# Four batches of sketch attention and routed expert attention: from stages with gaps to one written list for three engines

## The chip, the cores and the metric

The kernel runs on one core of one Trainium2 chip. The metric is the device time of one execution in microseconds (us). Engines are named as in the profile: PE is TensorE's matmuls and PEld its weight loads, DVE is VectorE, ACT is ScalarE, POOL is GpSimd and SP is SyncE, which here only issues DMAs.

## The reference

Inputs are q, k, v of (4 batches, 4 heads, 1088 rows, 32), two 8 x 32 sketch matrices S1 and S2 in 64-bit floats, and the weights of a routed attention layer with four experts of width 64. In outline:

```
a, b  = S1 x, S2 x                        # for every row x of q and of k
phi   = outer(a, b)                       # 64 features for one head
kv, z = sum_s phi(k) v, sum_s phi(k)
x     = phi(q) kv / (phi(q) z + 1e-6)     # heads side by side: 128 columns
logits = x @ w_gate;  the top 2 of 4 experts, softmax over the two
for each expert e:
    scores = x wq[e] (x wk[e])^T / 8, causal;  a = softmax(scores)
    ye = a (x wv[e]) wo[e]
    out += weight of e in this row * ye
```

## The kernel before

Rows are cut into nine tiles of 128 (tiles 0 to 7) and 64 (tile 8). One batch goes through these pieces, each a function of the kernel:

- `begin_k`, `begin_q`: DVE transposes of the loaded k and q. `sketch`: PE multiplies 64-row halves with the sketch weights `SKW`, which are split into a high and a low 32-bit part (NS is 2); the two parts accumulate in PSUM over two matmuls of 32 columns. ACT copies out, and one product makes the 64 features (`kp`, `qp`): on DVE in batch 0, on POOL afterwards.
- `kvs` sums phi(k) v over the rows. `turn_features` transposes the features of q on PE. `numer` multiplies and DVE divides, which gives `xs`; `turn_x` transposes it to `xT`. `spread_x` copies `xs` by 16 DMAs into `xrep`, the left operand of `values`.
- `gate`: one matmul of 4 columns for each tile, with the 128 columns of `xT` as the weights; then DVE finds the chosen two experts (`sel`), and `weights()` makes their shares (`gw`) with steps on DVE, POOL and ACT.
- `chosen`: x times all four expert matrices wq wk^T (512 columns), from which ACT copies two blocks and DVE overwrites parts by predicate, so that `u` holds for each row the vectors of its two chosen experts. `turn_chosen` transposes `u` to `uT`.
- `step` (and `last_step` for tile 8): the scores of both chosen experts, 128 i + 128 columns for tile i; DVE takes them out of PSUM with the mask and the minimum (`take`), ACT makes the exponentials and their sums (`soften`), and DVE transposes the weights block by block into `aT` (`turns`).
- `values`: for each block of 32 keys, four matmuls of 32 rows (one for each quarter of a block, each into its own PSUM bank) of `xrep` with `aT`. `keep` copies the sums to `yT` by one ACT instruction.
- `Out.heads`, `Out.turn`, `Out.put`: the value projections of the chosen experts, scaled on DVE (`hb`) and added on POOL; a PE transpose; the output projection, an ACT copy and the output DMAs.

Order. PE, DVE and ACT run each its instructions in the order in which the Python code emits them. For each batch the loop goes over six score steps, (4,2), (5,1), (3), (6,0), (7), (8). After each step's matmuls, takes and exponentials come the transposes of the step before, and then a list of other work for that gap (`gaps_of`): the output of the batch before, the sketches and features of the next. `values` of the groups B (tiles 4, 5) and C (tiles 1, 2, 3) stand in one gap, those of group A (0, 6, 7, 8) in the first gap of the next batch. The eight PSUM banks are divided: banks 0 to 3 belong to the scores alone, and `bank()` goes round banks 4 to 7 for all else; `values` takes all four of these.

Of the kernel before, what the change touches and what calls it, by code (L numbers as in the profile page):

```python
# [15 lines left out]
AX = mybir.AxisListType  # L16


@with_exitstack
def kernel(  # L20
# [15 lines left out]
    nc = tc.nc  # L36
# [145 lines left out]
    ident = const("ident", [128, 128])  # L184
    make_identity(nc, ident)
# [16 lines left out]
    GROUPS = {"B": (4, 5), "C": (1, 2, 3), "A": (0, 6, 7, 8)}  # L202
    COL = {"B": 0, "C": 128, "A": 0}
    KEPT = {"B": 0, "C": 4, "A": 10}
# [70 lines left out]
    def sketch(b, nm, j0, j1, eng):  # L275
# [5 lines left out]
        k0 = bank(2)  # L281
        for j in range(j0, j1):
            for m in range(2):
                for half in (0, 64):
                    rows, x = slice(64 * m, 64 * m + 64), 128 * j + half
                    for s in range(NS):
                        nc.tensor.matmul(P[half : half + 64, k0 + m, 32 * (j - j0) : 32 * (j - j0) + 32],  # L287
                                         xT_[rows, x : x + 64],
                                         SKW[rows].rearrange("p s x h r -> p (s x h r)")[:, 32 * s : 32 * s + 32],
                                         start=(s == 0), stop=(s == NS - 1))  # L290
        for m in range(2):
            t = P[:, k0 + m, 0 : 32 * (j1 - j0)].rearrange("p (j x d) -> p x j d", j=j1 - j0, x=2)
            nc.scalar.copy(ab[:, :, j0:j1, 2 * m : 2 * m + 2].rearrange("p x j h r -> p x j (h r)"), t)  # L293
# [62 lines left out]
    def gate(b, j0, j1):  # L356
        m_, k0 = batch(b), bank()
        for j in range(j0, j1):
            nc.tensor.matmul(P[:, k0, E * j : E * j + E], m_.xT[:, 128 * j : 128 * j + 128], wg, start=True, stop=True)
# [20 lines left out]

        def weights():
            V.reduce_max(top.rearrange("p j o -> p (j o)"), lg, axis=AX.X)
            G.tensor_tensor(out=w, in0=lg, in1=tops, op=ALU.subtract)
            nc.scalar.activation(out=w, in_=w, func=ACTF.Exp)
            G.tensor_tensor(out=w, in0=w, in1=ch, op=ALU.mult)
# [3 lines left out]
            G.tensor_tensor(out=w, in0=w, in1=tops, op=ALU.mult)  # L389
# [3 lines left out]
        return weights  # L393

    def chosen(b, i):
# [29 lines left out]
    def step(b, tiles):  # L425
# [8 lines left out]
        for s in range(2):  # L434
            for i in tiles:
                c, end = at[i], at[i] + 128 * i + 128
                while c < end:
                    n = min(end, c // 512 * 512 + 512) - c
                    nc.tensor.matmul(flat[:, 1024 * s + c : 1024 * s + c + n], m_.uT[:, i, s],  # L439
                                     m_.xT[:, c - at[i] : c - at[i] + n], start=True, stop=True)  # L440
                    c += n
        for s in range(2):
            for x, i in enumerate(tiles):
# [3 lines left out]
                take(a[:, s, cols], flat[:, 1024 * s + at[i] : 1024 * s + at[i] + n], mask[:, 1024 - n :], m)  # L447
                soften(a[:, s, cols], m, m_.z[:, i, s : s + 1])

        def turns():  # L450
            for i in tiles:
                n, u0 = blocks(i), unit(i)
                nc.vector.transpose(aT[GRP[i]][:, 0:n, u0 : u0 + 2].rearrange("p c s k -> p s c k"),  # L453
                                    a[:, :, at[i] : at[i] + 32 * n].rearrange("p s (c k) -> p s c k", k=32))

        return turns

    def last_step(b):

        m_, k0, i = batch(b), bank(), NJ - 1  # L460
# [237 lines left out]
```

## Time and profile before

| | us |
|---|---|
| three timed runs | 474.12, 480.95, 484.09 (median 480.95) |
| the profiled execution, its own time | 478.73 |
| its span, first to last instruction | 476.8 |
| PE, DVE, ACT, POOL busy | 381.3, 196.1, 136.7, 62.7 |

The profiled execution lies 2.2 us below the median, and 1.9 us of its time lie around its span. Busy is the time in which an engine's records run; a busy PE is not PE at its peak, since the granted clock has two levels (1.2 and 2.4 GHz) and was 0.846 of the upper one on average.

### The profile page before, as it was taken

To read this page: it belongs to the slowest core of one execution; us is meant where nothing else is said; L and a number is where in the kernel's file an instruction comes from. 1 tells how busy PE (TensorE), PEld (TensorE's weight loads), DVE (VectorE), ACT (ScalarE), POOL (GpSimd) and SP (SyncE) were. 2 spreads that over 40 slices of the span, in tenths; PEclk is the share of its full clock that TensorE was granted. 3 is DMA by queue.
4 is the path that set the end of the run, shared out by engine and by line. 5 is a ranking of instruction groups with operands and counts; after the bars stand their busy time and mean duration, and the time that the engine had idled before them with its cause. 6 is when DMAs were issued, how large, how long until landed. Compare 5 with 4: busy or idle time off the path is not lost.

```text
span 476.8 us, 12480 instructions
## 1 busy us (share of the span) xinstructions
PE 381.3 (80%) x5480; PEld 280.5 (59%) x5480; DVE 196.1 (41%) x527; ACT 136.7 (29%) x352; POOL 62.7 (13%) x132
## 2 busy tenths in 40 slices
PE   5978778698876977599788786789797787788795
PEld 2963433576653945368755763568574575367584
DVE  4334454442465054531663236512455416343601
ACT  2223142232325042231333232302422413423211
POOL 2010000430101001322011001124010100000101
PEclk9555787689889898979789897859978898889899
DMA  8410431110000080300000062000000025000000
GB/s 207 126 50 1 107 83 47 49 50 3 2 1 28 6 180 21 99 3 3 3 0 29 1 138 50 21 1 4 3 2 11 18 58 132 20 3 1 5 25 21
DMA packets 30326, 19.23 MB, mean 40 GB/s; under 512 B 5184, under 2 KB 29248, under 8 KB 30272
## 3 DMA queue, kind: packets, MB, share of 16 engines
q1 hardware_dynamic: 30256, 18.43, 15.6%
q8 instruction: 43, 0.70, 0.6%
q14 instruction: 11, 0.09, 0.1%
q10 hardware_dynamic: 16, 0.00, 0.0%
HBM read 7.28 MB, written 2.23 MB: 20 GB/s over the span
## 4 chain that ended last, share of the span: by engine, by line
PE 63%; DVE 18%; ACT 8%; issue 5%; POOL 3%; DMA 2%; SPq 0%; ACTq 0%; POOLq 0%; DVEq 0%
PE P L487 18%; PE P L439 16%; PE P L398 6%; PE P L531 5%; DVE a L419 5%; DVE u L408 5%; PE P L229 4%; PE P L325 3%; PE P L309 3%; PE P L287 3%; PE P L548 3%; ACT a L423 2%; DVE aTA L453 2%; POOL kp L296 2%; PE P L466 2%
## 5 line engine op out<-in xcount | busy, mean ns | idle before, releaser
L419 DVE CUSTOM_DVE_ANT_0 a<-P,mask 128x640 f32<-128x640 f32 (+4 forms) x64 | 46.6, 756 | 116.7 <-PE P L439 116.7
L439 PE MATMUL P<-xT,uT 128*128 128x512 f32 (+3 forms) x192 | 79.3, 567 | 1.4 <-ACT uT L230 1.4
L423 ACT ACTIVATE a<-a,mx 128x512 f32<-128x512 f32 (+8 forms) x68 | 54.0, 795 | 75.3 <-DVE mx L419 75.0
L408 DVE COPY_PREDICATED u<-sel,P 128x128 f32<-128x128 int32 x144 | 31.8, 293 | 68.3 <-ACT u L404 68.3
L439 PEld LDWEIGHTS P<-xT,uT 128*128 128x128 f32 x192 | 38.4, 221 | 32.1 <-issue 26.9
L398 PE MATMUL P<-mcat,xT 128*128 128x512 f32 x72 | 46.3, 749 | 8.1 <-DVE u L408 5.1
L487 PE MATMUL P<-aTA,xrep 32*128 32x160 f32 (+3 forms) x1080 | 44.0, 318 | 8.2 <-DVE r L511 8.2
L487 PEld LDWEIGHTS P<-aTA,xrep 32*128 32x128 f32 x1080 | 43.3, 204 | 10.5 <-ACT a L423 9.9
L531 PE MATMUL P<-wvx,yT 128*128 128x192 f32 (+1 forms) x144 | 39.0, 431 | 2.2 <-ACT yT L492 1.0
L537 POOL TENSOR_TENSOR hb<-hb 128x128 f32<-128x128 f32 (+1 forms) x36 | 16.3, 454 | 150.1 <-DVE hb L535 149.8
L531 PEld LDWEIGHTS P<-wvx,yT 128*128 128x128 f32 (+1 forms) x144 | 31.4, 244 | 5.8 <-issue 3.0
L492 ACT COPY yT<-P 128x1280 f32<-128x1280 f32 (+1 forms) x8 | 8.5, 1066 | 82.2 <-PE P L487 82.2
L535 DVE TENSOR_TENSOR hb<-P,gw 128x384 f32<-128x384 f32 (+1 forms) x36 | 19.1, 549 | 28.1 <-PE P L531 27.9
L229 PE MATMUL P<-ident,u 64*128 64x64 f32 x144 | 14.6, 272 | 17.8 <-DVE u L408 16.9
L229 PEld LDWEIGHTS P<-ident,u 64*128 64x128 f32 x144 | 9.0, 145 | 32.4 <-DVE u L408 15.1
L229 PEld LDWEIGHTS P<-ident,hb 64*128 64x128 f32 x144 | 7.7, 149 | 33.8 <-POOL hb L537 19.3
L229 PE MATMUL P<-ident,hb 64*128 64x64 f32 x144 | 11.9, 257 | 17.3 <-POOL hb L537 11.4
L487 PE MATMUL P<-aTB,xrep 32*128 32x128 f32 (+1 forms) x720 | 23.4, 272 | 2.8 <-ACT qab L293 2.8
L398 PEld LDWEIGHTS P<-mcat,xT 128*128 128x128 f32 x72 | 14.5, 226 | 17.5 <-issue 9.4
L487 PEld LDWEIGHTS P<-aTB,xrep 32*128 32x128 f32 x720 | 22.8, 187 | 3.3 <-ACT qab L293 3.1
L548 PE MATMUL P<-wo,hT 128*128 128x128 f32 (+1 forms) x144 | 21.8, 293 | 3.0 <-DVE u L408 3.0
L403 ACT COPY u<-P 128x128 f32<-128x128 f32 x36 | 9.4, 262 | 51.2 <-PE P L398 51.2
(116 smaller groups left out, 470.2 us busy)
## 6 DMA issues: line engine op xcount, KB each, us to landing
xrep<-xs SPq DMA_DIRECT2D x32, 144.0 KB, 3.3
xrep<-xs SPq DMA_DIRECT2D x32, 128.0 KB, 3.2
kin<-in_k_dram SPq DMA_DIRECT2D x4, 544.0 KB, 3.8
qin<-in_q_dram SPq DMA_DIRECT2D x4, 544.0 KB, 3.9
vin<-in_v_dram SPq DMA_DIRECT2D x16, 128.0 KB, 3.9
out_dram<-ob SPq DMA_DIRECT2D x32, 64.0 KB, 1.5
vtl<-in_v_dram SPq DMA_DIRECT2D x8, 16.0 KB, 2.4
wqk<-in_moe_wq_dram SPq DMA_DIRECT2D x1, 128.0 KB
```

What stands on the lines that cost most here:

```text
L229: nc.tensor.transpose(P[:, k0 + h, 64 * x : 64 * x + 64], a[rows], ident[rows, rows])
L287: nc.tensor.matmul(P[half : half + 64, k0 + m, 32 * (j - j0) : 32 * (j - j0) + 32], xT_[rows, x : x + 64], SKW[rows].rearrange("p s x h r ...
L398: nc.tensor.matmul(P[:, k0], m_.xT[:, 128 * i : 128 * i + 128], mcat.rearrange("p e d -> p (e d)"), start=True, stop=True)
L408: V.copy_predicated(u[:, s], m_.sel[:, i, 3 * s + x : 3 * s + x + 1].bitcast(I32).to_broadcast([128, DM]), c[:, x])
L419: nc.vector.tensor_tensor_reduce(out=dst, in0=src, in1=msk, scale=-1.0, scalar=most, op0=ALU.add, op1=ALU.min, accum_out=mx)
L423: nc.scalar.activation(out=a, in_=a, func=ACTF.Exp, bias=mx, scale=-1.0, accum_out=z)
L439: nc.tensor.matmul(flat[:, 1024 * s + c : 1024 * s + c + n], m_.uT[:, i, s], m_.xT[:, c - at[i] : c - at[i] + n], start=True, stop=True)
L487: nc.tensor.matmul(P[:, 4 + r, COL[grp] + 32 * us[0] : COL[grp] + 32 * len(units)], xrep[rows, c], aT[grp][rows, c, us[0] :], start=(c == ...
L531: nc.tensor.matmul(P[0:nq, k0, 64 * X * s : 64 * X * s + 64 * X], m_.yT[:, u, quarters].rearrange("p r q -> p (r q)"), wvx[:, X * s : X * ...
L535: nc.vector.tensor_tensor(out=hb[0:nq], in0=P[0:nq, k0, 0 : 2 * X * HD].rearrange("p (x d) -> p x d", d=HD), in1=m_.gw[0:nq, i, :, None].t ...
L537: nc.gpsimd.tensor_tensor(out=hb[0:nq, 1:3], in0=hb[0:nq, 1:3], in1=hb[0:nq, 4:6], op=ALU.add)
L548: nc.tensor.matmul(P[0:nq, k0, DM * t : DM * t + DM], self.hT[:, 2 * t + g, 0:nq], wo_sb[:, g], start=(g == 0), stop=(g == NG - 1))
```

## The change

The loop over batches, steps and gaps is replaced by `ORDER`, a written list of 321 words. A word is batch, task and arguments: `1.s:4:2` is the score step of tiles 4 and 2 of batch 1. The list sets the order of PE, DVE and ACT, from the first instruction on (`manual_schedule` now covers the setup too). Tasks: bk, bq = begin_k, begin_q; ks, qs = sketch of k, q; kv = kvs; tf = turn_features; nu = numer; tx = turn_x; sp = spread_x; ld = load_next; ga = gate, ge = its exponentials, gw = the rest of its weights; c = chosen; tu = turn_chosen; s = scores; t = transposes of one tile's weights; vb, va = a quarter of `values` of a group; sh = shares; h, ht, o = heads, turn, put. The first part of the list, two later places and its end:

```
0.bk 0.ks:0:4 0.vk 0.bq1 0.ks:4:9 0.bq0 0.em 0.kv 1.ld 0.qs:4:9 0.tf:13:18 0.tf:8:13 1.bk 0.qs:0:4 0.nu:4:9
0.tf:0:8 1.bq 0.tx:4:9 0.nu:0:4 1.ks:4:9 1.ks:0:4 0.tx:0:4 0.sp 2.ld 0.ga:0:4 0.ge:0 0.c:2 0.c:3 0.c:1 1.kv
0.tu:2:3 2.bk 1.qs:4:9 0.c:0 1.qs:0:4 0.s:3 0.gw:0 2.bq 1.tf:8:13 0.tu:0:1 0.t:3 0.ga:4:9 1.tf:0:8 0.c:5 0.c:4
1.tf:13:18 2.ks:0:4 0.c:7 0.ge:4 1.nu:0:5 0.tu:4:5 0.c:6 0.c:8 0.s:5:1 0.s:4:2 1.nu:5:9 0.tu:6:7 0.tu:8 0.t:1
0.t:2 2.ks:4:9 1.tx:4:9 0.t:5 1.tx:0:4 0.s:7 0.t:4 2.kv 2.qs:4:9 2.qs:0:4 0.s:8 0.s:6:0 0.gw:4 2.tf:8:13 0.t:6
0.t:0 0.sh:0:6 3.ld 0.t:7 0.t:8 0.vb:0 2.tf:13:18 0.vb:1 0.vb:2 0.vb:3 1.ga:0:9 2.tf:0:8 0.h:4 0.va:0 1.c:3 0.va:1
...
3.sp 3.t:4 2.sh:0:6 3.t:1 3.s:7 2.h:3 3.s:8 2.h:0 2.h:4 3.s:6:0 3.vb:0 3.vb:1 3.t:6 2.ht:0 3.t:0 2.sh:6:9 3.vb:2
...
3.t:8 2.o:6 3.va:0 3.gw:0 2.o:8 3.va:1 3.sh:0:6 3.h:4 3.va:2 3.sh:6:9 3.h:3 3.va:3 3.h:2 3.ht:3 3.h:1 3.h:5 3.o:3
3.ht:1 3.h:8 3.ht:5 3.o:1 3.h:6 3.h:7 3.ht:8 3.o:5 3.h:0 3.ht:6 3.o:8 3.ht:0 3.o:6 3.o:0
```

Besides the order: `bank()` takes of all eight banks the one (or the aligned pair) that was used longest ago, except banks that a running `values` holds. Groups B and C become one group B (tiles 1 to 5), `values` runs in four parts of a group (words vb:0 to vb:3), and four copies, two on ACT and two on DVE, take its sums out. `aT` is kept in two parts for each group, so that a tile's transpose becomes up to two. `sketch` multiplies by both parts of `SKW` at once (64 columns) and DVE adds the halves. `gate` uses 32 columns of `xT` as weights in place of 128. `chosen` makes one ACT copy and two wider predicated copies. The add of `heads` and small steps of `weights` and `shares` move from POOL to DVE.

The core of the diff:

```diff
     def bank(n=1):
-        k = turn[0] % 4
-        if n == 2 and k % 2:
-            k = (k + 1) % 4
-        turn[0] = k + n
-        return 4 + k
+        k = min((k for k in range(0, 8, n) if not held & set(range(k, k + n))), key=lambda k: max(used[k : k + n]))
+        used[k : k + n] = [max(used) + 1] * n
+        return k
+    ctx.enter_context(tc.manual_schedule(
+        engines={mybir.EngineType.PE, mybir.EngineType.DVE, mybir.EngineType.Activation}))
...
-    GROUPS = {"B": (4, 5), "C": (1, 2, 3), "A": (0, 6, 7, 8)}
+    GROUPS = {"B": (1, 2, 3, 4, 5), "A": (0, 6, 7, 8)}
+    CUT = {"B": 16, "A": 4}
...
-                    for s in range(NS):
-                        nc.tensor.matmul(P[half : half + 64, k0 + m, 32 * (j - j0) : 32 * (j - j0) + 32],
-                                         xT_[rows, x : x + 64],
-                                         SKW[rows].rearrange("p s x h r -> p (s x h r)")[:, 32 * s : 32 * s + 32],
-                                         start=(s == 0), stop=(s == NS - 1))
+                    nc.tensor.matmul(P[half : half + 64, k0 + m, w * (j - j0) : w * (j - j0) + w], xT_[rows, x : x + 64],
+                                     SKW[rows].rearrange("p s x h r -> p (s x h r)"), start=True, stop=True)
...
+            nc.scalar.copy(o, t[:, 0])
+            if NS == 2:
+                nc.vector.tensor_tensor(out=o, in0=t[:, 1], in1=o, op=ALU.add)
...
-            nc.tensor.matmul(P[:, k0, E * j : E * j + E], m_.xT[:, 128 * j : 128 * j + 128], wg, start=True, stop=True)
+            for r in range(4):
+                x = 128 * j + 32 * r
+                nc.tensor.matmul(P[32 * r : 32 * r + 32, k0, E * j : E * j + E], m_.xT[:, x : x + 32], wg,
+                                 start=True, stop=True)
...
-        nc.scalar.copy(u[:, 0], c[:, 0])
-        nc.scalar.copy(u[:, 1], c[:, 3])
+        nc.scalar.copy(u, c[:, 0:4:3])
...
+            f = 512 * bank(2 if base > 512 else 1)
...
+    PARTS = {"B": (0, 4, 8, 14, 24), "A": (0, 7, 14, 21, 34)}
+    def values(b, grp, part):
+        if part == 0:
+            k0 = bank(2)
+            held.update((k0, k0 + 1))
+            k1 = bank(2)
+            held.update((k1, k1 + 1))
+            sums[grp] = k0, k0 + 1, k1, k1 + 1
...
+            for r in range(4):
+                (nc.scalar.copy, nc.vector.tensor_copy)[r % 2](
+                    batch(b).yT[:, KEPT[grp] : KEPT[grp] + n, r],
+                    P[:, sums[grp][r], 0 : 32 * n].rearrange("p (u q) -> p u q", q=32))
...
-            nc.gpsimd.tensor_tensor(out=hb[0:nq, 1:3], in0=hb[0:nq, 1:3], in1=hb[0:nq, 4:6], op=ALU.add)
+            nc.vector.tensor_tensor(out=hb[0:nq, 1:3], in0=hb[0:nq, 1:3], in1=hb[0:nq, 4:6], op=ALU.add)
...
+    for word in ORDER.split():
+        b, task = word.split(".")
+        name, *args = task.split(":")
+        TASKS[name](int(b), *map(int, args))
```

## Rows read from the trace of the kernel before

**Rows 1.** The page: busy time, share of the span and instructions of each engine.

```profile
PE 381.3 (80%) x5480; PEld 280.5 (59%) x5480; DVE 196.1 (41%) x527; ACT 136.7 (29%) x352; POOL 62.7 (13%) x132
```

**Rows 2.** Span and mean granted clock of the core.

```profile
core 0: 476.8 us, clock 0.846
```

**Rows 3.** Stages: length, busy (instructions) of PE, PEld, DVE, ACT, POOL; granted clock, DMA.

```profile
0.00:42.00 42.00, 30.98 (x493) 22.97 (x493) 17.09 (x57) 9.41 (x24) 5.80 (x25) 0.62 0.41 109
42.00:103.00 61.00, 47.10 (x562) 28.58 (x563) 28.09 (x85) 19.04 (x59) 7.74 (x14) 0.73 0.26 65
103.00:213.00 110.00, 87.01 (x1364) 65.41 (x1364) 46.92 (x123) 33.18 (x88) 17.11 (x29) 0.91 0.15 37
213.00:325.00 112.00, 92.73 (x1364) 69.64 (x1364) 46.32 (x121) 32.84 (x85) 15.42 (x26) 0.85 0.11 26
```

**Rows 4.** Waits of PE: for whom, us in total, times, longest.

```profile
PE P L229 <- DVE u L408: 16.9, 15, 2.9
PE P L229 <- POOL hb L537: 11.4, 8, 2.6
PE P L309 <- POOL kp L296: 8.8, 6, 2.7
PE P L487 <- DVE r L511: 8.2, 3, 2.7
PE P L229 <- ACT qpT L230: 7.6, 3, 2.5
```

**Rows 5.** Short stretches inside the period of batch 2, columns as in rows 3.

```profile
306.00:316.50 10.50, 8.57 (x220) 8.24 (x220) 2.29 (x2) 1.30 (x5) 4.34 (x2) 0.53 0.01 3
316.50:322.00 5.50, 5.50 (x15) 2.99 (x12) 1.31 (x4) 0.72 (x2) 0.00 (x0) 0.65 0.00 0
325.30:336.00 10.70, 10.65 (x297) 10.52 (x298) 0.00 (x0) 0.27 (x2) 4.33 (x3) 1.00 0.02 5
```

**Rows 6.** PE in order of time: start, us, line, shape, count, idle before.

```profile
203.73 0.83 PE L309 MATMUL P<-vp,kp 128*64 128x33 f32 x12
204.49 5.28 PE L439 MATMUL P<-xT,uT 128*128 128x512 f32 x12
...
218.62 4.56 PE L487 MATMUL P<-aTC,xrep 32*128 32x192 f32 x111
...
242.57 2.17 PE L359 MATMUL P<-wg,xT 128*128 128x4 f32 x18
...
259.18 3.62 PE L439 MATMUL P<-xT,uT 128*128 128x512 f32 x12
...
306.43 4.10 PE L287 MATMUL P<-SKW,kT 64*64 64x32 f32 x144
...
313.41 3.20 PE L309 MATMUL P<-vp,kp 128*64 128x33 f32 x56 [1.55 <-POOL kp L296]
...
322.03 2.36 PE L287 MATMUL P<-SKW,qT 64*64 64x32 f32 x144
```

**Rows 7.** Groups by line: count, busy us, mean ns of one, idle before.

```profile
L398 PE MATMUL P<-mcat,xT 128*128 128x512 f32 x72 | 46.3, 749 | 8.1 <-DVE u L408 5.1 <-ACT yT L492 3.0
L408 DVE COPY_PREDICATED u<-sel,P 128x128 f32<-128x128 int32 x144 | 31.8, 293 | 68.3 <-ACT u L404 68.3
L537 POOL TENSOR_TENSOR hb<-hb 128x128 f32<-128x128 f32 (+1 forms) x36 | 16.3, 454 | 150.1 <-DVE hb L535 149.8
...
L325 PE MATMUL P<-kvz,qpT 64*64 64x33 f32 x576 | 13.9, 263 | 2.3 <-ACT qpT L230 2.1
...
L332 DVE TENSOR_TENSOR xs<-P,den 128x256 f32<-128x256 f32 (+1 forms) x16 | 6.6, 453 | 0.5
...
L371 DVE TENSOR_TENSOR eq<-eq,lower 128x144 f32<-128x144 f32 (+2 forms) x5 | 1.4, 278 | 0.2
```

**Rows 8.** SP in order of time, 160 to 200 us, columns as in rows 6.

```profile
165.41 11.81 SPq L220 DMA_DIRECT2D xrep<-xs  x16
```

More of the change, by code (lines that the diff above doesn't have):

```diff
@@ L468, in last_step @@
         take(a[:, 1024:], P[:, k0, 0:64], mask_last, mx[:, 0, 0:1])
[L469 removed]
+        take(a[:, 0:1024], flat[:, 512 * k1 : 512 * k1 + 1024], mask[:, 0:1].to_broadcast([128, 1024]), mx[:, 0, 1:2],
+             mx[:, 0, 0:1])
         soften(a, mx[:, 0, 1:2], m_.z[:, i, 0:1])
[L472 to L477 removed]
+        left[b, i] = a[:, None, :]
+    PARTS = {"B": (0, 4, 8, 14, 24), "A": (0, 7, 14, 21, 34)}
+    sums = {}
+    def values(b, grp, part):
         tiles, units = GROUPS[grp], UNITS[grp]
+        if part == 0:
[4 more added lines that the diff above has]
+            sums[grp] = k0, k0 + 1, k1, k1 + 1
         last = {(i, r): min(4 * i + r, NC - 1) for i in tiles for r in range(4)}
[L481 removed]
+        for c in range(*PARTS[grp][part : part + 2]):
+            (c0, _, u0), t = next((p, t) for p, t in zip(parts(grp), aT[grp]) if p[0] <= c < p[1])
             for r in range(4):
@@ L640, with gate_ @@
-    with tc.manual_schedule(engines={mybir.EngineType.PE, mybir.EngineType.DVE, mybir.EngineType.Activation}):
-        first_part()
-        load_next(1)
-        left = None
-        for b in range(B):
-            tiles = TILES if b else [(3,), (4, 2), (5, 1), (6, 0), (7,), (8,)]
-            gaps = gaps_of(b)
-            for n, t in enumerate(tiles):
-                turns = last_step(b) if t == (8,) else step(b, t)
-                if left:
-                    left()
-                left = turns
-                if n == 0 and b:
-                    shares(b - 1, 0, 1)
-                    shares(b - 1, 6, 8)
-                    last_shares(b - 1)
-                if n == 3:
-                    shares(b, 1, 6)
-                for f in gaps[n]:
-                    f()
-        left()
-        b = B - 1
-        shares(b, 0, 1)
-        shares(b, 6, 8)
-        last_shares(b)
-        values_a(b)
-        for f in outs(b, (0,), (6, 7), (8,)):
-            f()
+    def gate_(b, j0, j1):
+        weights[b, j0] = gate(b, j0, j1)
@@ new lines, in scores, with warm @@
+    def scores(b, *tiles):
+        if tiles == (NJ - 1,):
+            last_step(b)
+        else:
+            step(b, tiles)
+    def warm(b, n):
+        k0 = bank()
+        for _ in range(n):
+            nc.tensor.matmul(P[:, k0], ident, ident[:, None, :].to_broadcast([128, 4, 128]), start=True, stop=True)
+    TASKS = {
+        "bk": begin_k, "bq": lambda b: begin_q(b, 0, C), "bq0": lambda b: begin_q(b, 0, C // 2),
+        "bq1": lambda b: begin_q(b, C // 2, C), "vk": values_of_k, "em": lambda b: expert_matrices(),
+        "ks": lambda b, j0, j1: sketch(b, "k", j0, j1, G if b else V), "qs": lambda b, j0, j1: sketch(b, "q", j0, j1, G if b else V),
+        "kv": kvs, "tf": turn_features, "nu": numer, "tx": turn_x, "ga": gate_, "ge": lambda b, j: weights[b, j][0](), "gw": lambda b, j: weights[b, j][1](),
+        "sp": spread_x, "ld": load_next, "ldn": lambda b: load_next(b + 2), "c": choose,
+        "tu": lambda b, *t: turn_chosen(b, [us[b, i] for i in t], t[0]),
+        "s": scores, "t": turn_weights, "vb": lambda b, part: values(b, "B", part), "va": lambda b, part: values(b, "A", part),
+        "sh": shares,
+        "h": lambda b, i: out_of(b, *PAIRS[i]).heads(i), "ht": lambda b, i: out_of(b, *PAIRS[i]).turn(),
+        "o": lambda b, i: out_of(b, *PAIRS[i]).put(), "warm": warm,
+    }
```

225 lines of the change are left out of this document (86 added, 139 removed).

## The prediction

> **What bounds the kernel now.** I read the busy table first [rows 1]. PE is busy for 80% of the span, DVE for 41%, ACT and POOL for less, so PE is the only engine that can bound the whole; DMA shares of 0.11 to 0.41 in the stages [rows 3] leave it out. But PE loses time in two ways. It is idle for 476.8 - 381.3 = 95.5 us [rows 1, 2]. And its mean granted clock was 0.846 [rows 2]: with two levels, a share of 2 x (1 - 0.846) = 0.31 of the span, 147 us, ran at the lower one. The same twelve score instructions took 3.62 us at one place and 5.28 at another, the same 144 sketch instructions 2.36 and 4.10 [rows 6], so most work on PE pays for the clock. If PE was busy for 0.8 of those 147 us, half of that, about 59 us, is the clock's price. PE's work at the full clock is then about 381 - 59 = 322 us, two thirds of the span.
>
> Next, the waits of PE by cause [rows 4]. They are many and short: 15 waits for the chosen vectors `u`, 8 for POOL's add into `hb`, 6 for POOL's features `kp`. The reader should see in them a chain through three or four engines, with too little other work standing in the list behind it. DVE and ACT are no bottleneck there; they wait as well. The stages [rows 3] show where it is worst: 0 to 42 us, at clock 0.62, and 42 to 103, at 0.73 with 14 us of PE idle. The short stretches [rows 5] show the clock's pattern: 0.53 where PE ran sketches and key sums with waits between them, 0.65 in the scores that followed, and 1.00 in `values`, where PE ran on without a gap.
>
> **The change part by part.** I make the sum against the profiled execution: span 476.8, its own time 478.73, which is 2.2 below the median of the three runs.
>
> *Sketches.* 1,152 sketch matmul instructions become 576 of twice the columns. If the instruction's own rate bounds them, half of their time goes: today 4.10 us for 144 at the low clock and 2.36 at the high [rows 6], 6.5 us a batch, so 12 us over four batches, counting a little for less overlap. If the columns bound them, nothing goes. The nearest row, the weighted key sums, has 56 instructions of 33 columns with twice the weight rows in 3.20 us, 57 ns each, against 28 for a sketch [rows 6]: what the weights bring counts, and their number halves here. I take -8 (0 to -12). DVE gets 32 adds out of PSUM.
>
> *Gate.* 18 instructions took 2.17 us, 0.12 each, for four columns [rows 6]; that is the load of 128 columns of weights, since the columns are few. They become 72 with a quarter of the weight columns. At a sketch's 16 ns each that is 1.2 us a batch, at the 57 ns of the key sums 4.1. So four batches give -4 to +8; I take -3, nearer to the sketch, which also loads few columns in several places at once.
>
> *Values.* Joining B and C removes the matmuls of C (116 instructions a batch, 111 of them in 4.56 us [rows 6]); their columns are added to those of B. Their columns alone, taken at the rate of the joined work, need some 3.3 us. I take -1.3 a batch, -5 in all (0 to -8). The four copies that take the sums out cost ACT about what one does now and DVE 16 x 0.42, near the 0.453 us of the division out of PSUM [rows 7].
>
> *Chosen.* 144 predicated copies become 72 of twice the width: DVE 31.8 us [rows 7] falls to about 26, if one costs between 0.29 and 0.59. *Adds of `hb`*: 36 x 0.454 us leave POOL, and 36 x 0.278 (a like product [rows 7]) come to DVE, 10 us. Transposes in two parts add 20 instructions and some 3 us. With the 32 sketch adds (9 us), the copies (7) and the gate's small steps (3) DVE goes from 196 to 196 - 6 + 10 + 3 + 9 + 7 + 3 = 222 us, at most 235. That is still under 60% of what follows, so these go at nothing on the path. Their cover is PE's own work in the list, and where it is missing, each is one wait of 0.3 to 0.6 us.
>
> PE's work at the full clock: 322 - 8 - 3 - 5 = 306 us (bounds 290 to 330).
>
> *The order.* This is the large term. Between a chain's parts the list now puts other work of PE. After 0.c:3 stand 0.c:1 and 1.kv before 0.tu:2:3 needs `u`: one chosen matmul pair at 1.3 us (46.3 / 36 [rows 7]) and 72 key sums, 4 us, against 1.1 us for the copy and the predicated ones. Between 1.ks and 1.kv, where POOL needs its features and PE now waits for up to 2.6 us [rows 4], stand a transpose, a gate and three chosen. The 95.5 us of idle time should shrink to about 43: 10 at the start and the end (first loads, last output), 8 in the first hundred us, where DVE gets the front parts of three batches at once, and 25 for all else, about a third of today's. What is late next there is DVE itself, in order: a `take` that waits for its scores holds up the `hb` and `u` queued behind it, and PE waits for those.
>
> *Where DMAs move.* 2.ld stands behind 0.sp on SP. The 16 copies of 0.sp take SP 11.81 us to issue [rows 8], while the list has some 8 us of PE work between 0.sp and 2.bk. So 2.bk, first in DVE's order, holds DVE for some 5 to 8 us, with 1.qs and the copies on ACT to cover it. 3.sp may start only when 2.va:3 is done, since `xrep` has one copy. The list has about 11 us of scores and heads before 3.vb:0, so a wait of about 4 us is left. Both are in the 33 us above.
>
> *Clock.* Up to the first `values` the work is that of today's first 103 us, at 0.62 to 0.73 [rows 3], plus small matmuls of batches 1 and 2; I keep 0.68 for 54 us of work, which costs 25. For the rest I take 0.95, against 0.85 to 0.91 today [rows 3], because fewer waits stand between large matmuls: 240 to 252 us of work costs 12. Together 36.
>
> *A rule against the change.* PE changes the shape of its matmuls (128*64 to 128*128, say) at almost every word. In the trace the scores at 204.49 begin before the key sums before them end, at 203.73 + 0.83 [rows 6], so I price a change of shape at nothing; ends of matmuls are modelled, so this row is weak. The Trainium skill, TensorEngine Tiling (Array Packing), section Tiling Modes, Key Properties, says that a change of the tiling mode drains TensorE. By that rule the sum would be higher, and a rival below prices it from rows.
>
> Sum: 306 + 36 + 43 = 385 us of span, and 1.9 around it: 387.
>
> **The rivals.** *The waits stay.* In-order queues on three engines only trade one late engine for another, and idle time stays near 95. For it: 40% of DVE's time is busy now, and PE still waits. Against it: the covers counted above. 306 + 50 + 95 + 2 = 453 us.
>
> *DVE becomes the bound in places.* With 222 us on an in-order queue, unevenly spread, and the two DMA waits growing, idle time is 75 rather than 43: about 418 us. For it: the front parts of three batches come first, and nothing on DVE may pass a late `2.bk`.
>
> *A change of shape costs time.* If each of the 168 changes in the list drained PE for as long as one small matmul's record lasts, 263 ns [rows 7], 44 us come on top, less what today's changes already cost: 425 us. The rule is that of the paragraph above.
>
> *Slower: the clock falls.* Today the full clock holds where PE runs ten us of `values` and the scores after it [rows 5]. The list cuts `values` into four parts and mixes small matmuls between all large ones. If that kept the mean clock at the 0.62 to 0.65 seen in the first stage and after the key sums [rows 3, 5], 306 / 0.65 = 471 us of PE and 30 idle would give 503. It decides below a mean clock of 0.69, where 306 / c + 43 passes 489. Against it: 103 to 213 us, where small and large are mixed too, had 0.91 [rows 3]. The Trainium skill, TensorE: Matmul & The Clock Gate, section "A second HAM failure mode: psum-queue depth-cycling", says that PE's short idle times between groups of matmuls, in a kernel that goes round the PSUM banks, made the clock swing between its levels; going round all eight banks is what this change does. The stretch at 0.53 with its waits agrees [rows 5].
>
> **How the numbers follow.** The forecast 0.60, DVE in places 0.17, waits that stay 0.12, the clock 0.07, shapes 0.04. The range of 348 to 432 holds the forecast with its bounds (PE's work 290 to 330, waits 30 to 60), the DVE case and the shapes. Within 2% (471 to 491; the three runs spread by 2% too) ends a part of the waits that stay, 0.05; the rest of that case is faster. Faster 0.88, same 0.05, slower 0.07.
>
> **What would show it.** PE busy share near 90%, idle below 50; the list of PE's waits without POOL; the first `values` near 100 us; clock 0.88 to 0.93, with 0.95 after 100 us; sketch instructions halved in number at less than 1.5 times the time of one. Wrong would be: a clock below 0.8 behind 100 us, DVE busy all through a stretch while PE waits, or long waits for `xrep` or `2.bk`.

## The result and the profile after

The changed kernel took 328.95 us, the median of four runs (327.21 to 330.09); the kernel before, on the same chip, 482.52 (474.12 to 485.07). The ratio is 0.6885, with a 95% interval of 0.6787 to 0.6984. Every ratio in this document compares fast executions alone and leaves out slower ones at a lower clock, which is why 0.6885 is not the quotient of these two medians, and why run 1 leaves out an execution of 528.20 us at a mean clock of 0.608. The forecast was 387 with a range from 348: the direction was right, and the gain was underestimated by 58 us. The profiled execution took 328.93 us, 1.8 of them around its span.

The page of the changed kernel (compare [rows 1]); below it PE's busy tenths and its granted clock in 40 slices of 8.2 us.

```profile
PE 307.9 (94%) x4656; PEld 222.8 (68%) x4656; DVE 231.9 (71%) x574; ACT 129.9 (40%) x324; POOL 38.9 (12%) x61
...
PE   7559996999999999999999999999999999999994
...
PEclk9755599699999999999999999999999999999999
```

Span and mean clock (compare [rows 2]).

```profile
core 0: 327.1 us, clock 0.947
```

Stages, with the columns of [rows 3].

```profile
0.00:42.00 42.00, 31.60 (x594) 23.47 (x596) 27.13 (x69) 11.24 (x29) 10.43 (x27) 0.67 0.61 161
42.00:103.00 61.00, 57.48 (x1021) 39.53 (x1018) 50.23 (x130) 28.50 (x70) 16.56 (x15) 0.94 0.20 49
103.00:213.00 110.00, 109.32 (x1743) 78.96 (x1743) 83.92 (x215) 48.18 (x123) 10.50 (x13) 1.00 0.21 49
213.00:300.00 87.00, 86.50 (x961) 60.98 (x963) 62.00 (x138) 36.24 (x88) 1.18 (x5) 1.00 0.16 37
300.00:327.20 27.20, 22.99 (x359) 19.84 (x351) 8.65 (x23) 5.68 (x15) 0.23 (x1) 0.99 0.10 28
```

The reader should see the step at 42 us. In the first stage the two kernels look alike: 10 to 11 us idle in each, clock 0.62 before and 0.67 now. From 103 to 300 us PE is idle for 1.2 us of 197 and its clock is 1.00, where before 23 of 110 us were idle at 0.91.

What is left of PE's waits (compare [rows 4]):

```profile
PE P L273 <- DVE qp L348: 3.3, 1, 3.3
PE P L338 <- DVE kT L314: 2.9, 1, 2.9
PE P L377 <- DVE u L462: 2.4, 1, 2.4
PE P L403 <- ACT wT L274: 1.6, 1, 1.6
PE P L155 <- DVE mcat L132: 1.1, 1, 1.1
PE P L273 <- POOL qp L348: 1.1, 2, 0.7
```

Each of these six lies in the first 60 us, while the first batch's chain fills. The repeated waits for `u`, `hb` and `kp` are gone, and POOL is left with 1.1 us. PE in order of time shows the single sizes (columns as in [rows 6]):

```profile
57.27 2.36 PE L377 MATMUL P<-kvz,qpT 64*64 64x33 f32 x80 [2.42 <-DVE u L462]
...
79.94 1.28 PE L338 MATMUL P<-SKW,qT 64*64 64x64 f32 x72
...
83.13 3.72 PE L494 MATMUL P<-xT,uT 128*128 128x512 f32 x12
...
87.24 2.44 PE L544 MATMUL P<-aTB,xrep 32*128 32x320 f32 x32
...
97.18 0.78 PE L413 MATMUL P<-wg,xT 128*32 128x4 f32 x72
```

The groups of lines (compare [rows 7]) hold the clock's gain on instructions that did not change in number or shape: scores (L494), `chosen` (L455) and heads (L579). L462 and L544 are changed operations, which are taken up further down.

```profile
L494 PE MATMUL P<-xT,uT 128*128 128x512 f32 (+3 forms) x192 | 66.1, 493 | 0.0
L455 PE MATMUL P<-mcat,xT 128*128 128x512 f32 x72 | 39.6, 669 | 0.0
L544 PE MATMUL P<-aTB,xrep 32*128 32x320 f32 (+4 forms) x720 | 39.2, 350 | 0.0
L462 DVE COPY_PREDICATED u<-sel,P 128x256 f32<-128x256 int32 x72 | 30.7, 443 | 18.9 <-ACT u L459 17.5
L579 PE MATMUL P<-wvx,yT 128*128 128x192 f32 (+1 forms) x144 | 30.1, 339 | 0.3 <-DVE xs L384 0.3
```

Before, `chosen` took 46.3 us [rows 7], and scores and heads:

```profile
L439 PE MATMUL P<-xT,uT 128*128 128x512 f32 (+3 forms) x192 | 79.3, 567 | 1.4 <-ACT uT L230 1.4
L531 PE MATMUL P<-wvx,yT 128*128 128x192 f32 (+1 forms) x144 | 39.0, 431 | 2.2 <-ACT yT L492 1.0 <-DVE u L408 0.7 <-ACT hT L230 0.5
```

### The profile page after: what moved, and what is told of

It reads as the page before. It is cut to its first block, busy times and chain, and to the rows that moved or that the text cites. A ratio compares the mean times of both kernels' runs of the same rounds, so it can differ in the third digit from the quotient of the medians.

```text
span 327.1 us, 10742 instructions
## 1 busy us (share of the span) xinstructions
PE 307.9 (94%) x4656; PEld 222.8 (68%) x4656; DVE 231.9 (71%) x574; ACT 129.9 (40%) x324; POOL 38.9 (12%) x61
## 4 chain that ended last, share of the span: by engine, by line
PE 87%; DVE 8%; DMA 3%; ACT 1%; issue 1%; DVEq 0%; ACTq 0%
PE P L544 24%; PE P L494 20%; PE P L455 10%; PE P L579 8%; PE P L273 7%; PE P L596 5%; PE P L338 3%; PE P L361 3%; PE P L377 3%; PE P L515 2%; DVE aTB L257 1%; DMA vtl<-in_v_dram 1%; DMA kin<-in_k_dram 1%; DVE qT L318 1%; PE P L413 1%; DVE kp L348 1%
## 5 line engine op out<-in xcount | busy, mean ns | idle before, releaser
L477 ACT ACTIVATE a<-a,mx 128x896 f32<-128x896 f32 (+8 forms) x68 | 53.9, 793 | 50.5 <-DVE mx L473 50.1
L494 PE MATMUL P<-xT,uT 128*128 128x512 f32 (+3 forms) x192 | 66.1, 493 | 0.0
L473 DVE CUSTOM_DVE_ANT_0 a<-P,mask 128x768 f32<-128x768 f32 (+4 forms) x64 | 46.0, 752 | 12.2 <-PE P L494 11.7
L494 PEld LDWEIGHTS P<-xT,uT 128*128 128x128 f32 x192 | 33.5, 191 | 26.2 <-issue 18.8
L462 DVE COPY_PREDICATED u<-sel,P 128x256 f32<-128x256 int32 x72 | 30.7, 443 | 18.9 <-ACT u L459 17.5
L544 PEld LDWEIGHTS P<-aTA,xrep 32*128 32x128 f32 x1080 | 38.2, 185 | 4.2 <-issue 3.3
L544 PE MATMUL P<-aTA,xrep 32*128 32x160 f32 (+3 forms) x1080 | 40.8, 297 | 0.0
L455 PE MATMUL P<-mcat,xT 128*128 128x512 f32 x72 | 39.6, 669 | 0.0
L544 PE MATMUL P<-aTB,xrep 32*128 32x320 f32 (+4 forms) x720 | 39.2, 350 | 0.0
L544 PEld LDWEIGHTS P<-aTB,xrep 32*128 32x128 f32 x720 | 33.9, 185 | 5.0 <-issue 0.8
L579 PE MATMUL P<-wvx,yT 128*128 128x192 f32 (+1 forms) x144 | 30.1, 339 | 0.3 <-DVE xs L384 0.3
L579 PEld LDWEIGHTS P<-wvx,yT 128*128 128x128 f32 (+1 forms) x144 | 22.4, 184 | 6.3 <-issue 2.7
L257 DVE STREAM_TRANSPOSE aTA<-a 128x256 f32<-128x256 f32 (+4 forms) x28 | 24.5, 918 | 1.0 <-ACT a L477 1.0
L257 DVE STREAM_TRANSPOSE aTB<-a 128x1024 f32<-128x1024 f32 (+3 forms) x28 | 24.4, 911 | 0.9 <-ACT a L477 0.9
L459 ACT COPY u<-P 128x256 f32<-128x256 f32 x36 | 13.0, 372 | 20.1 <-PE P L455 19.6
L455 PEld LDWEIGHTS P<-mcat,xT 128*128 128x128 f32 x72 | 13.4, 206 | 10.6 <-issue 8.4
L596 PEld LDWEIGHTS P<-wo,hT 128*128 128x128 f32 (+1 forms) x144 | 17.7, 185 | 3.3 <-issue 1.4
L348 POOL TENSOR_TENSOR kp<-kab 128x1280 f32<-128x1280 f32 (+1 forms) x6 | 13.0, 2171 | 32.7 <-DVE kab L345 32.5
```

The source lines that it names most:

```text
L257: nc.vector.transpose(t[:, 0 : c1 - c0, n - u0 : n - u0 + s].rearrange("p c s k -> p s c k"), a[:, :, 32 * c0 : 32 * c1].rearrange("p s (c ...
L348: eng.tensor_tensor(out=fp[:, j0:j1].rearrange("p j h (x y) -> p (j h) x y", y=R), in0=a_[:, 1, :, None, :].to_broadcast([128, n, R, R]), ...
L455: nc.tensor.matmul(P[:, k0], m_.xT[:, 128 * i : 128 * i + 128], mcat.rearrange("p e d -> p (e d)"), start=True, stop=True)
L462: nc.vector.copy_predicated(u, sel[:, :, x, None].to_broadcast([128, 2, DM]), c[:, x, None, :].to_broadcast([128, 2, DM]))
L473: nc.vector.tensor_tensor_reduce(out=dst, in0=src, in1=msk, scale=-1.0, scalar=most, op0=ALU.add, op1=ALU.min, accum_out=mx)
L477: nc.scalar.activation(out=a, in_=a, func=ACTF.Exp, bias=mx, scale=-1.0, accum_out=z)
```

## The experiments

The theory: PE's waits at the ends of chains cost twice, as idle time and as a fallen clock, and the written order with free banks removes both. The rivals: the cheaper operations did it, or the banks did.

**1. The old order, in words.** `ORDER` names the tasks in the order of the kernel before; everything else is the changed kernel.

```diff
-    0.bk 0.ks:0:4 0.vk 0.bq1 0.ks:4:9 0.bq0 0.em 0.kv 1.ld 0.qs:4:9 0.tf:13:18 ...
+    0.bk 0.bq0 0.vk 0.ks:0:4 0.ks:4:9 0.bq1 0.em 0.kv 0.qs:0:4 0.tf:0:8 0.nu:0:4 ...
```

> The changed kernel with the order of before, written as a list of its own words (parts of values one behind the other, eight banks and all new operations stay). Theory 1, the order closes the gaps and thereby keeps the clock: PE idle 80 to 95 us again, mean clock 0.84 to 0.88, 450 to 460 us, that is before less the 18 to 25 us of PE work saved by the operations. Theory 2, the banks and the cheaper operations did most of it: PE idle below 50, under 400 us.

Measured: 444.45 to 448.12 us, ratio 0.9408 (0.9314 to 0.9501): most of the gain is gone.

**2. The old order and the divided banks.** On top of it the scores get banks 0 to 3 and all else 4 to 7, as before; what is left of the change are the operations.

```diff
-        k = min((k for k in range(0, 8, n) if not held & set(range(k, k + n))), key=lambda k: max(used[k : k + n]))
-        used[k : k + n] = [max(used) + 1] * n
-        return k
+        k = turn[0] % 4
+        if n == 2 and k % 2:
+            k = (k + 1) % 4
+        turn[0] = k + n
+        return 4 + k
...
-            f = 512 * bank(2 if base > 512 else 1)
+            f = 1024 * s
```

> As old_order, and with the banks divided as before (0 to 3 for scores, 4 to 7 in turn for the rest and for values). Theory 1: within 2% of old_order, so eight banks are worth nothing without the order. Rival, banks in order of age lift waits by themselves: over 10 us slower than old_order.

Measured: ratio 0.9953 (0.9902 to 1.0004); the profiled execution took 471.48 us. Its page:

```profile
PE 355.1 (76%) x4656; PEld 255.0 (54%) x4656; DVE 226.6 (48%) x582; ACT 131.7 (28%) x324; POOL 38.1 (8%) x65
```

and its longest waits of PE:

```profile
PE P L277 <- DVE u L466: 19.5, 18, 3.2
PE P L277 <- DVE hb L582: 12.6, 10, 3.5
PE P L365 <- POOL kp L352: 12.5, 6, 4.9
PE P L277 <- DVE hb L584: 10.0, 5, 2.5
```

This is the row to learn from. PE does the same job with 381.3 - 355.1 = 26 us less busy time, and by the ratio the time stays. Of the 26 us, 19 are idle time now: the span is 469.7 us, so 114.6 are idle in place of 95.5. (The other 7 are the difference between the two traced spans, 476.8 and 469.7; the ratio, from executions side by side, has 2.) What PE saves, it waits for at the end of the same chains. So the operations alone are refuted. The expectation that the banks are worth nothing without the order failed too: between run 1 and this one lie 26 us.

**3. The new order with the old operations.** Sketches, gate, `chosen`, the small steps of `weights` and the add of `hb` as before (for instance):

```diff
-            nc.vector.tensor_tensor(out=hb[0:nq, 1:3], in0=hb[0:nq, 1:3], in1=hb[0:nq, 4:6], op=ALU.add)
+            nc.gpsimd.tensor_tensor(out=hb[0:nq, 1:3], in0=hb[0:nq, 1:3], in1=hb[0:nq, 4:6], op=ALU.add)
```

> The changed kernel in its new order, with five operations as before: sketches of two accumulated 32-column matmuls, the gate with 128 weight columns, two copies and four predicated copies for the chosen vectors, the add of the heads and three steps of the gate's weights on POOL. Theory 1: PE work grows by some 15 us at the full clock (sketches 9, gate 5) and the covers hold: 343 us, idle of PE below 30, clock above 0.93. Rival, the shorter chains on DVE and POOL make the order work: idle above 45, over 360 us.

Measured: 345.76 us, ratio 0.7274 (0.7196 to 0.7351); the profiled execution, the fastest, took 341.44. Its page:

```profile
PE 324.7 (96%) x5016; PEld 241.7 (71%) x5016; DVE 204.2 (60%) x563; ACT 132.5 (39%) x360; POOL 57.2 (17%) x112
```

Here these operations (all that changed but the joined `values`, the transposes in two parts and `shares`) are worth 345.8 - 329.0 = 17 us by the medians and 19 by the ratios; PE is busy for 94 to 96% of the span in both kernels, so what it saves counts. A part of this is clock. Twice in this trace the clock falls while PE has no gap, at 99.80 and at 174.90 us, and both times the old gate, 18 instructions with 128 weight columns and 4 columns, has just run; the changed kernel has no such fall. For the second one, the gate in order of time, and the stretches before and behind the fall with the columns of [rows 3]:

```profile
172.66 2.17 PE L410 MATMUL P<-wg,xT 128*128 128x4 f32 x18
```

```profile
168.00:174.90 6.90, 6.90 (x122) 6.16 (x116) 1.11 (x2) 0.00 (x0) 2.91 (x3) 1.00 0.00 0
174.90:185.14 10.24, 10.24 (x193) 9.67 (x195) 2.86 (x12) 0.70 (x3) 2.80 (x2) 0.50 0.02 3
```

So waits are not the only thing that the clock falls behind. That it was the gate, and not the small matmuls next to it, no run shows by itself.

The ladder from the kernel before goes by ratios, from 1 to 0.9953, 0.9408 and 0.6885. Of some 475 us the operations bring 2, within what the interval leaves open, the free banks 26 and the order 120. These parts hold for this sequence of steps: the operations, put in last, bring 17 to 19, and the new order with the banks divided four and four was not run.

**4. The trace of the old order.** One more execution of the kernel of run 1.

> The kernel of old_order once more, for an undisturbed trace: 444 to 449 us; PE idle between the 95 us of before and the 115 of the divided banks if the banks' gain is fewer waits, clock 0.84 to 0.88.

Measured: 444.74 us, with clock 0.857 and this page:

```profile
PE 346.0 (78%) x4656; PEld 248.6 (56%) x4656; DVE 226.2 (51%) x582; ACT 130.3 (29%) x324; POOL 38.2 (9%) x65
```

Idle are 442.9 - 346.0 = 96.9 us, as many as before the change. This is the kernel that my rival of waits that stay described (453).

**5. Joined `values` cut in two.** Columns of B are multiplied in two matmuls, as B and C were.

```diff
+                    cut = max(us[0], 6) if grp == "B" else us[0]
+                    for x, y in ((us[0], cut), (cut, len(units))):
```

> The changed kernel with each matmul of the joined group cut again into two, for tiles 1 to 3 and for tiles 4 and 5 (58 matmuls a batch more, the same columns). The prediction's step, 1.3 us a batch saved by joining: 333 to 335 us. Rival, the columns bound these matmuls and joining saved nothing: within 1% of the changed kernel, 327 to 331 us.

Measured: 331.15 us (330.95 to 331.29), ratio 0.6984 (0.6925 to 0.7043): joining is worth 2 us by the medians and 5 by the ratios, whose intervals overlap a little. PE's own time for the matmuls of B, all at the upper clock level here and in the changed kernel, says more: 44.1 against 39.2 us, that is the 5 of the forecast.

```profile
L547 PE MATMUL P<-aTB,xrep 32*128 32x128 f32 (+2 forms) x1184 | 44.1, 288 | 0.1
```

**6. Old sketches alone.** The two halves are again accumulated in PSUM, without DVE's add.

```diff
-                                     SKW[rows].rearrange("p s x h r -> p (s x h r)"), start=True, stop=True)
+                                     SKW[rows].rearrange("p s x h r -> p (s x h r)")[:, 32 * s : 32 * s + 32],
+                                     start=(s == 0), stop=(s == NS - 1))
```

> The changed kernel with the sketches of before (two accumulated matmuls of 32 columns, no DVE add). The term of the prediction, 8 us of PE work, 9 by the rows after: 336 to 339 us if PE is the bound throughout. Rival, the start is bound by DVE, where the adds are saved: 330 to 333 us.

Measured: 333.84 us (331.81 to 337.09), ratio 0.6965 (0.6888 to 0.7041). Beside the repeated changed kernel on the same chip (run 8) that is 6 us by the ratios, near the 8 forecast, though the intervals touch.

**7. The add of `hb` on POOL.** The edit shown in run 3, alone.

> The changed kernel with the add of the heads back on POOL: 36 x 0.34 us leave DVE, and the chain to the transpose gets longer by some 0.3 us. Theory 1, DVE has slack and the order covers the chain: within 0.7% of the control. Rival, DVE at 71% is the next bound: 1% to 2% faster. Second rival, the add's place on DVE matters: over 1% slower.

Measured: 328.52 us, ratio 0.6865 (0.6828 to 0.6901): no difference. DVE's added work is covered, as the prediction had it.

**8. The changed kernel again,** for runs 6, 7 and 9.

> The changed kernel itself, on the chip of the three runs below, so that differences of 1% can be read: 327 to 330 us by every theory.

Measured: 327.96 us, ratio 0.6848 (0.6789 to 0.6907).

**9. `values` in one piece.** The four parts of a group stand together at the place of the last.

```diff
-    ... 0.vb:0 2.tf:13:18 0.vb:1 0.vb:2 0.vb:3 1.ga:0:9 2.tf:0:8 0.h:4 0.va:0 1.c:3 0.va:1 1.c:2 1.c:5 0.va:2 ...
+    ... 2.tf:13:18 0.vb:0 0.vb:1 0.vb:2 0.vb:3 1.ga:0:9 2.tf:0:8 0.h:4 1.c:3 1.c:2 1.c:5 1.tu:2:3 0.va:0 0.va:1 ...
```

> As values_whole, but with the four parts gathered at the place of the last one, so that the heads of the batch before still read their own sums and the result is the reference's. Theory 1, the parts are cover for other chains: PE idle up by 10 to 20 us and the clock below 0.95, 338 to 350 us. Rival, the overlap of batches alone suffices: within 1.5% of the control.

Measured: 337.06 us (335.04 to 339.18), ratio 0.7047 (0.6977 to 0.7116), clock 0.939. Cutting `values` into parts and filling between them is worth 9 us. The prediction had named that cutting as a reason for a falling clock; it does the opposite: from 72 to 300 us the clock is 0.98 without it and 1.00 with it. An earlier form had all four parts at the place of the first:

> The changed kernel with the four parts of each values word list moved together, so that values of a group runs in one piece of about 10 us again; all else in the new order. Theory 1, the parts are cover for the chains of chosen vectors and heads: PE idle up by 10 to 20 us, 338 to 350 us, with the clock still over 0.9. Rival, the overlap of batches alone suffices: within 1.5%, 327 to 334 us.

It took 349.3 us, ratio 0.7334 (0.7275 to 0.7392). There the heads of tiles 6 to 8 of batch 0 read sums of the next batch, so run 9 is the one that counts.

**10. Six banks in rotation.** Banks 6 and 7 are only for `values`.

```diff
-        k = min((k for k in range(0, 8, n) if not held & set(range(k, k + n))), key=lambda k: max(used[k : k + n]))
+        k = min((k for k in range(0, 6, n) if not held & set(range(k, k + n))), key=lambda k: max(used[k : k + n]))
```

> The changed kernel with banks 6 and 7 kept for values, so that all other work goes round six banks by oldest use and, while values run, four. Theory 1, the order leaves enough work between two uses of a bank: within 1.5% of the changed kernel, 327 to 334 us. Rival, the free choice of banks is what lets the order run (dividing them cost 29 us in the old order): over 340 us, with waits of PE for ACT and DVE copies out of PSUM.

Measured: 341.17 to 341.54 us in three executions, at a mean clock of 0.930, and 336.05 in a fourth, at 0.954; run 8 on the same chip has 327.96. So two banks less cost some 8 to 13 us. In the trace, of 341.34 us, PE is idle for 24 us in place of 19, and the clock from 103 to 213 us is 0.97 in place of 1.00. The expectation that the order leaves enough work between two uses of a bank (327 to 334) failed.

**11 to 13. What lowers the clock.** At one place of the middle stage, behind 2.c:1, one of three things is put in: 216 small matmuls of 64 x 64 weights and 33 columns, nine of 512 columns, or nine adds on DVE with one matmul behind them that needs them. Their results are not used. (The trace has two records for each matmul.) The edit is that of the first; the others put 2.warm:9 and 2.pause:9 there.

```diff
-    ... 1.h:2 2.c:1 2.c:8 ...
+    ... 1.h:2 2.c:1 2.small:54 2.c:8 ...
```

> The changed kernel with 216 added small matmuls (64 rows, 64 weight columns, 33 columns, no input from other engines) in one run in the middle of the list, before the words 2.c:8, where PE has no gaps and the clock is 1.00. Their results are not used. At the 16.4 ns of an instruction they are 7 us. Theory A, only waiting lowers the clock: clock stays at 1.00 in and behind them, 336 us. Theory B, a run of small matmuls lowers it without any wait: clock 0.5 to 0.6 in its later part and in the large matmuls behind it, 340 to 346 us.

> The changed kernel with 9 added matmuls of 512 columns at the same place, results not used: 7.7 us at the full clock. Both theories: clock 1.00 throughout, 336 to 337 us.

> The changed kernel with nine added DVE products of 512 elements (about 0.65 us each) at the same place and one matmul that needs the last of them, results not used, so that PE waits some 6 us. Theory A: the clock falls to 0.5 during or behind the wait, 336 to 342 us. Theory B: a pause of this length alone does little, clock back at 1.00 at once, 333 to 335 us.

Measured: 341.28, 337.97 and 339.49 us, one execution each. Short windows of the small ones, columns as in [rows 3]:

```profile
189.00:192.00 3.00, 1.98 (x135) 1.87 (x128) 0.97 (x3) 0.00 (x0) 0.00 (x0) 1.00 0.03 5
192.00:195.00 3.00, 3.00 (x128) 2.95 (x128) 0.00 (x0) 0.00 (x0) 0.00 (x0) 0.61 0.02 5
195.00:198.00 3.00, 2.64 (x100) 2.57 (x100) 0.00 (x0) 0.00 (x0) 0.00 (x0) 0.50 0.02 5
...
204.00:207.00 3.00, 3.00 (x25) 1.96 (x22) 0.95 (x3) 1.66 (x3) 0.00 (x0) 0.61 0.00 0
207.00:210.00 3.00, 3.00 (x13) 2.11 (x12) 2.45 (x6) 0.59 (x2) 0.00 (x0) 1.00 0.00 0
```

of the large ones:

```profile
195.00:198.00 3.00, 3.00 (x9) 1.33 (x8) 0.00 (x0) 0.00 (x0) 0.00 (x0) 1.00 0.02 5
```

and of the pause:

```profile
189.00:192.00 3.00, 0.00 (x0) 0.00 (x0) 2.86 (x6) 0.00 (x0) 0.00 (x0) 1.00 0.00 0
192.00:195.00 3.00, 0.00 (x0) 0.00 (x0) 2.86 (x5) 0.00 (x0) 0.00 (x0) 0.54 0.00 0
...
204.00:207.00 3.00, 3.00 (x9) 1.73 (x8) 1.63 (x4) 0.74 (x2) 0.00 (x0) 0.68 0.00 0
```

Through the large matmuls the clock stays at 1.00. Behind a wait of 8.05 us it falls to 0.50, and it falls in the run of small ones too: PE was busy for 1.98 of the 3 us before the window of the fall, and for 88 to 100% of the two windows from there on. Both are back at 1.00 only at 207 us. By the shares 0.61 and 0.54 of the window where the clock falls and 0.61 and 0.68 of the one where it rises, each spent nearly 14 us at the lower level. The small run had issue gaps of 1.02 and 0.36 us of its own, the first right before the fall, so this run cannot tell the gap from the small matmuls; the two falls of run 3 had no gap.

**14 to 16. Filling the start.** Eight large matmuls whose results are not used stand in PE's three longest early waits; then five more between the small words of the start; then, with the first eight, the gate's comparisons read one operand from PSUM.

```diff
-    0.bk 0.ks:0:4 ... 0.qs:4:9 0.tf:13:18 ... 0.ge:4 1.nu:0:5 ...
+    0.bk 0.warm:3 0.ks:0:4 ... 0.qs:4:9 0.warm:3 0.tf:13:18 ... 0.ge:4 0.warm:2 1.nu:0:5 ...
...
-        theirs = lg[:, :, None, :].to_broadcast([128, m, E, E])
+        theirs = P[:, k0, E * j0 : E * j1].rearrange("p (j e) -> p j e", e=E)[:, :, None, :].to_broadcast([128, m, E, E])
```

> The changed kernel with eight added 512-column matmuls, results not used, in the three longest waits of PE in the first 60 us (before 0.ks:0:4, 0.tf:13:18 and 1.nu:0:5). If the waits there keep the clock down: 320 to 326 us, with the clock of the first 42 us up from 0.67 to 0.8. If the small matmuls keep it down: 328 to 333 us, clock unchanged.

> As warm_fill with five more single large matmuls between the small words of the first 40 us. If large matmuls among small ones hold the clock: clock of the first 42 us at 0.85 or more, 317 to 325 us. If they only cost their time: 332 to 338 us.

> The kernel of warm_fill, with the two comparisons of the gate reading one of their operands from PSUM in place of SBUF. In the changed kernel the second comparison took 1.98 us in place of 0.22 while POOL made a feature product. If two operands in SBUF are what waits for POOL, the comparison takes 0.2 to 0.3 us at the same place and the product with two SBUF operands behind it (eq with lower, 0.23 us) takes the wait, 1 to 2 us; the time stays within 0.7% of warm_fill, 324 to 328 us. If DVE as a whole is slowed by POOL: the comparison keeps its 2 us.

Measured: 326.36 us (ratio 0.684, 0.6788 to 0.6892), 327.18 (0.6868, 0.6811 to 0.6925) and 325.96 (0.6914, 0.6823 to 0.7005). With the eight fillers the clock of the first 42 us rises from 0.67 to 0.88:

```profile
0.00:42.00 42.00, 34.36 (x634) 22.48 (x635) 26.75 (x70) 11.25 (x30) 10.84 (x28) 0.88 0.62 161
```

yet the time moves by about 2 us, no more than the intervals leave open; the 320 to 326 and 317 to 325 us expected for the first two were missed. PE in order of time in run 14 (L633 are the fillers) shows where the gain goes:

```profile
19.85 4.91 PE L633 MATMUL P<-ident 128*128 128x512 f32 x6
...
41.94 0.34 PE L274 MATMUL P<-ident,u 64*128 64x64 f32 x4 [1.27 <-DVE u L463]
```

The fillers themselves delay the transposes of `qp`, which begin behind them at 24.69 us, from 23.55 in the changed kernel. Those of `u`, which began at 42.87 there without a wait, are ready to start at 40.67 here and wait 1.27 us for DVE. So the faster PE is held up by its fillers and by DVE. Which of the two counts for more was not separated. These versions lie below the changed kernel by the median, but not clearly.

## Why the prediction was low

Right were the direction, the mechanism and what was to be seen: PE's share is 94% (near 90% was said), idle 19.2 us (below 50), waits without POOL but for 1.1 us, the first `values` at 87 us (near 100). The mean clock, 0.947, lies just above what was to be seen (0.88 to 0.93). DVE is busy for 231.9 us (222, at most 235), and that costs nothing (run 7). Of the two DMA waits, for `2.bk` and for `xrep` before 3.vb:0, neither is among PE's waits.

*Operations.* 72 sketches of 64 columns take 1.28 us, 18 ns each, against 16 for the old ones of 32 [rows 6]: nearly the instruction's rate sets their time, as I took it. The gate takes 0.78 us for a batch against 2.17, so -5.6 in all in place of -3. Joined `values` took 4.9 us off PE, as forecast with 5 (run 5). Predicated copies of twice the width went from 293 to 443 ns, so `chosen` gave DVE 1 us back and not 6. These errors are small.

*The sum.* It had three terms, and all three were too high. To take PE's busy time apart, add it up over the stretches in which the granted clock was at the lower level: in the changed kernel, in the kernel before and in run 2.

```profile
sum 34.13, PE 28.07 PEld 22.46 DVE 24.68 ACT 8.00 POOL 9.02; mean PE 14.04 PEld 11.23 DVE 12.34 ACT 4.00 POOL 4.51
sum 146.76, PE 131.91 PEld 97.87 DVE 47.53 ACT 18.44 POOL 19.91; mean PE 6.00 PEld 4.45 DVE 2.16 ACT 0.84 POOL 0.90
sum 143.36, PE 117.77 PEld 85.17 DVE 58.92 ACT 20.41 POOL 23.18; mean PE 6.93 PEld 5.01 DVE 3.47 ACT 1.20 POOL 1.36
```

Half of that busy time is taken as the clock's price, as in the prediction. So the changed kernel pays 14 us, and its work at the full clock is 307.9 - 14 = 294. The same sum gives 355.1 - 59 = 296 for run 2, which has the same operations at a much lower clock, so the half is near enough. Against the forecast: PE's work 294, where I had 306; clock 14, where I had 36; idle 327.1 - 307.9 = 19, where I had 43. The gap of 385 - 327 = 58 us is 12 + 22 + 24.

*The first step that failed* is "25 for all else, about a third of today's". I had no row for that third. Behind 103 us PE is idle for about 5 us, 4 of them in the last 27. I had counted covers at two places of the list and then discounted them; I did not count the others, so that counting would have given the right size is not shown.

*The second* is the clock's term: "for the rest I take 0.95" and "0.68 for 54 us of work, which costs 25". From 64 to 300 us the clock is 1.00, so the 12 us for the rest came to nothing, and the start cost 14 in place of 25, since the clock was 0.94 from 42 to 103 us. (As worded, the two parts make 38 and not 36.) The clock is not a term of its own beside the idle time: run 13 shows that one wait of 8 us brings nearly 14 us at the lower level, some 10 of them while PE works again. I took the waits down and left most of the clock's loss in place; the two should have been priced together.

*The third* is the price of the clock today, "0.8 of those 147 us". By the sum above PE was busy for 131.9 of them, 0.90, so the price is 66 and not 59, and the work of the kernel before 315 and not 322. That is 7 of the 12 us. The other 5 are operations, which saved 21 us of work in place of 16: the gate 5.6 in place of 3, the sketches 9 (303 against 294 by the same sum in run 6) in place of 8, and some 1 to 2 us that the sum leaves open. The same working shows what run 2 gave back: 315 - 296 = 19 us less work, 19 us more idle time. The unchanged groups show the clock's price as well: scores 66.1 against 79.3, `chosen` 39.6 against 46.3, heads 30.1 against 39.0, 29 us on those three alone.

*Missing* was a term for the banks. In the old order they are worth 26 us, in the new one two of eight are worth 8 to 13 (run 10).

*The rivals.* "The waits stay" is true of the old order alone (run 4). "DVE becomes the bound" is refuted by run 7 and the list of waits, but for the start: the wait of 2.42 us at 57.27 ends with a `u` that DVE's queue held up, and run 14 meets DVE there too. "A change of shape costs time" has no room: from 103 to 300 us PE is idle for 1.2 us in all while shapes change at nearly every word. The drain that the Trainium skill states (TensorEngine Tiling (Array Packing), Tiling Modes, Key Properties) thus showed no price here, unless it hides inside the records. "The clock falls": a wait lowers it (run 13), and it fell without one behind the old gate (run 3); from 64 to 300 us the changed kernel shows no fall. The Trainium skill (TensorE: Matmul & The Clock Gate, "A second HAM failure mode: psum-queue depth-cycling") tells of a clock that swings through short idle times of PE in a kernel that goes round the banks. Here going round all eight banks left PE nearly without idle time, 1.2 of 197 us, and the clock at 1.00; with six in rotation it is lower, 0.97 in the middle stage.

## What to carry to other kernels

Where in-order engines wait at the ends of chains, cheaper operations can be given back as longer waits (here 19 us less of PE's work, 19 us more idle). First find an order in which each chain has other work behind it, and buffers that let it start; then the same savings count (17 us). Price idle time and TensorE's clock together, since a wait also costs what the engine does at the lower clock after it, and read the busy time at each clock level from the trace before pricing the clock. Cut long runs of work into parts that can fill waits (9 us here).

## What was not expected of the hardware

Small operations on DVE with both operands in SBUF were held until a POOL product beside them ended. Such an operation of the gate takes 0.23 us alone. In the changed kernel, DVE in order of time, the first line beside POOL and the second behind it:

```profile
36.79 1.98 DVE L425 TENSOR_TENSOR eq<-lg 128x64 f32<-128x64 f32 x1
38.88 0.23 DVE L426 TENSOR_TENSOR eq<-eq,lower 128x64 f32<-128x64 f32 x1
```

and POOL's two feature products beside it, which end at 38.70:

```profile
34.40 4.30 POOL L348 TENSOR_TENSOR kp<-kab 128x1280 f32<-128x1280 f32 x2 [10.75 <-DVE kab L345]
```

In run 16, where a comparison reads one operand from PSUM, it is free of that, and the next two with both in SBUF wait in its place, under POOL's two products from 34.22 to 38.52:

```profile
35.51 0.23 DVE L425 TENSOR_TENSOR gt<-P,lg 128x64 f32<-128x64 f32 x1
35.66 0.21 DVE L426 TENSOR_TENSOR eq<-P,lg 128x64 f32<-128x64 f32 x1
35.97 0.72 DVE L427 TENSOR_TENSOR eq<-eq,lower 128x64 f32<-128x64 f32 x1
36.72 1.87 DVE L428 TENSOR_TENSOR gt<-gt,eq 128x64 f32<-128x64 f32 x1
```

The Trainium skill (SBUF — State Buffer, "Who interferes with whom") says that a DVE instruction with two SBUF inputs contends with a GpSimd instruction that reads SBUF, and that one with at most one SBUF input does not, outside the two-port modes; 1.98, 0.72 and 1.87 against 0.21 to 0.23 us agree with it. No run here shows that it costs time in the whole: run 16 took 325.96 us, run 14 326.36.
